# Third weight chunk split by halves, and the second batch's first exponentials ahead of a worker's step, in a kernel of attention and two layers of matmuls

## The chip, the cores and the metric

The kernel runs on one core of a Trainium2 chip. The metric is the time of one execution on the device, in microseconds (us), taken as the median of several runs. The engines are named as the profile names them: PE is TensorE (matmuls; PEld its weight loads), DVE is VectorE, ACT is ScalarE, POOL is GpSimd, SP is SyncE, which here only issues loads and stores. PSUM is the memory that PE writes its accumulators to, in banks.

## What is computed

Sparse attention (the first half of the heads local, the other half strided), then a bilinear layer, then four experts weighted by given probabilities:

```python
def _attn_ref(q, k, v):                      # (2, 8, 576, 64) each
    scores = scale * np.matmul(q, k.transpose(0, 1, 3, 2))
    mask_local = (rel >= 0) & (rel < stride)
    mask_strided = (rel >= 0) & (pos[None, :] % stride == pos[:, None] % stride)
    ...
    scores = np.where(masks[None, :, :, :], scores, -1000000000.0)
    scores = scores - np.max(scores, axis=-1, keepdims=True)
    attn = np.exp(scores)
    attn = attn / (np.sum(attn, axis=-1, keepdims=True) + 1e-09)
    return np.matmul(attn, v).astype(np.float32)

def _moe_ref(x, w1, w2, w3, w_out):          # x (1152, 512), w1, w2 (512, 1024)
    return ((x @ w1) * (x @ w2) @ w3 @ w_out).astype(np.float32)

def _moe2_ref(x, domain_probs, w1, w2):
    p = domain_probs / (domain_probs.sum(-1, keepdims=True) + 1e-09)
    for e in range(E):
        out += p[:, e:e + 1] * (np.maximum(x @ w1[e], 0.0) @ w2[e])
    return out.astype(np.float32)
```

## The kernel before

The order of the instructions on every engine is the order in which the program is written. Each engine works through its own list in that order; semaphores make an instruction wait for what it reads.

**Matmuls in pairs.** Most operands are held as a rounded high part and the rest, `w_hi` and `w_lo`, `x_hi` and `x_lo`. One product step is three matmuls (`mm3`, lines 303 to 307): high by high, high weight by low x, low weight by high x.

**Weight chunks and the worker.** The weights of the bilinear layer come in chunks of 128 x 1024 (`Chunk`; eight of w1 and w2 in `c_w12`, then w_out and w3). Each is loaded as raw 64-bit words and made into numbers in steps: `magnitude` (line 149, ACT), `clamp`, `shift`, `sign`, `add` (lines 185 to 195, DVE) with `round_up` (line 144, ACT), then `split_hi` (line 203, a cast on ACT that writes `w_hi`) and `split_lo` (line 232, a subtraction on DVE that writes `w_lo`). The add ends with the load of a later chunk into the raw buffer that it has read. A generator `work` holds these steps from the third chunk on, each chunk's split mixed with the next one's steps; `advance(1)` issues what stands up to the next `yield`. The second chunk, made outside of it, already has its add and its split by halves (`add_halves`, `low_halves`, lines 207 to 220).

**Units.** The layer's first products are made in 32 units (batch, chunk, half of the batch's 576 tokens). A unit (`ab_block`, line 586) fills two PSUM accumulators of 128 x 288, w = 0 and w = 1, of twelve matmuls each. ACT copies the first to the tile `ab` (line 609), and DVE multiplies the second by it (line 611). The accumulator w = 0 reads columns 0 to 511 of the chunk, w = 1 the others. `run_unit` (line 889) issues a unit in two blocks, one for each accumulator, and after each block one step of the worker. Units 0 and 1 are made otherwise; units 2 and 3 read the second chunk, units 4 and 5 the third, units 6 and 7 the fourth.

**The second batch's attention** runs between the units, chunk by chunk (`Chunk4`, six of them), by `attend` (line 908). For chunk s a call makes: the scores of chunk s + 1 on PE (from the fourth on; the first three were made before), the maxima of chunk s (line 409 on DVE, scaled on GpSimd, line 411), the reciprocal and multiplication of chunk s - 1 (lines 453 and 457, DVE), values and output of chunk s - 3, and the transposes of chunk s - 2 (line 462, PE, tile `tp`). The exponentials of chunk s (line 433, six or eight on ACT) are put into the list `waiting` and issued in the next unit, after its first block and the worker's step. The scores lie in three PSUM banks, so the fourth chunk's scores take over the first one's bank. Before the change, the first call comes after unit 3, the second after unit 4, the third, which has the fourth chunk's scores and the first one's transposes, after unit 5.

**The rest** of the kernel, from 62 us on, is the other units, the product of w3 and w_out, and the experts.

Of the kernel before, what the change touches and what calls it, by code (L numbers as in the profile page):

```python
# [8 lines left out]
F32 = mybir.dt.float32  # L9
# [5 lines left out]
ALU = mybir.AluOpType  # L15
# [3 lines left out]
P = 128  # L19
# [25 lines left out]
def kernel(  # L45
# [13 lines left out]
    nc = tc.nc  # L59
    mm = nc.tensor.matmul  # L60
# [13 lines left out]
    def bank(name):  # L74
        return ps.tile([P, 512], F32, tag="ps", name=name)
# [54 lines left out]
    class Chunk:  # L130
# [68 lines left out]
        def split_hi(self):  # L199
            nonlocal live  # L200
            live += 2
            self.hi, self.lo = unit("w_hi"), unit("w_lo")
            nc.scalar.copy(self.hi, self.f32)
# [5 lines left out]
        def add_halves(self):  # L209
# [3 lines left out]
            for i in range(2):  # L213
                c = slice(512 * i, 512 * i + 512)
                self.add_half(i)
                nc.scalar.copy(self.hi[:, c], self.f32[:, c])

        def low_halves(self):
            for c in (slice(0, 512), slice(512, 1024)):
                nc.vector.tensor_tensor(out=self.lo[:, c], in0=self.f32[:, c], in1=self.hi[:, c].bitcast(F32),  # L220
                                        op=ALU.subtract)
            self.done = True

        def split_half(self, i, src):
            if i == 0:
# [5 lines left out]
        def split_lo(self):  # L231
            nc.vector.tensor_tensor(out=self.lo, in0=self.f32, in1=self.hi.bitcast(F32), op=ALU.subtract)
            self.done = True
# [8 lines left out]
    c_w12 = [Chunk(w12[c]) for c in range(8)]  # L242
    c_wout = [Chunk(w_out[c]) for c in range(4)]
    c_w3 = [Chunk(w3T[c]) for c in range(8)]
    live = 6
# [6 lines left out]
    def load_next(held=False):  # L252
        nonlocal loaded
        if loaded < len(stream):
            stream[loaded].raw_load(held)
            loaded += 1
            for load in rest_loads.pop(loaded, ()):
                load()

    def work():  # L260


        wide = stream[2:20]
        before = None
        for c, after in zip(wide, wide[1:] + [None]):
            if before:
                while live > 14:
                    yield False
                before.split_hi()
            c.clamp()  # L270
            yield True
            if before:
                before.split_lo()
            c.shift()
            yield True
            c.round_up()
            c.sign()
            yield True
            if after:
                after.magnitude()  # L280
            c.add()
            yield True
            before = c
        while live > 14:
            yield False
        before.split_hi()
        yield True
        before.split_lo()
        yield True
        for w in c_e:  # L290
            yield from w.work()

    worker = work()

    def advance(n=1):

        return all([next(worker, False) for _ in range(n)])

    def need(c, part=0):
        while not (c.done if part == 0 else c.done1 if part == 1 else c.done2):  # L300
            assert advance()

    def mm3(acc, lhs, rhs, first, last):
        (lh, ll), (rh, rl) = lhs, rhs
        mm(acc, lh, rh, start=first, stop=False)  # L305
        mm(acc, lh, rl, start=False, stop=False)  # L306
        mm(acc, ll, rh, start=False, stop=last)  # L307


    x_hi = xp.tile([P, 4, NT], F32R, tag="x_hi", name="x_hi")  # L310
    x_lo = xp.tile([P, 4, NT], F32R, tag="x_lo", name="x_lo")
# [218 lines left out]
    def ab_place(b, pair):  # L530
        both = big[b].tile([P, 4 * S], F32R, tag="big", name="ab_parts")
        parts_of[b, pair] = both[:, :4 * MAIN].rearrange("p (x k n) -> p x k n", x=2, k=2)
        rest = both[:, 4 * MAIN:].rearrange("p (x n) -> p x n", x=2)
        if pair == 3 and b == 0:
            middle[pair, 0] = rest[:, :, MID // 2:]
        elif pair == 3:
            nc.scalar.copy(rest[:, :, :MID // 2], middle[pair, 0].bitcast(F32))
        middle[pair, 1 - b] = rest

    def ab_pieces(b, ft, t0, n):  # L540
        pair, k = ft // 2, ft % 2
        pieces = []
        cut = MAIN if b == 0 else MID // 2
        for a, z in ((t0, min(cut, t0 + n)), (max(cut, t0), t0 + n)):
            if a < z:
                at = slice(a - t0, z - t0)
                if (a < cut) == (b == 0):
                    off = 0 if b == 0 else cut
                    pieces.append((at, parts_of[b, pair][:, :, k, a - off:z - off]))
                else:  # L550
                    off = b * S - MAIN
                    pieces.append((at, middle[pair, k][:, :, a + off:z + off]))
        return pieces
# [32 lines left out]
    def ab_block(b, ft, n):  # L586
        t = slice(b * S + n * HB, b * S + n * HB + HB)
        pair, late = ft // 2, b == 0 and ft < 6
        ab = tmp.tile([P, HB], F32, tag="pT", name="ab")
        if n == 0 and ft % 2 == 0:  # L590
            if late:
                if pair < 2:
                    parts = big[pair].tile([P, 2, 2, S], F32, tag="big", name="ab_f32")
                    whole[pair] = parts[:, 0]
                    if pair:
                        whole[2] = parts[:, 1]
            elif (b, pair) not in parts_of:
                ab_place(b, pair)
        if late:
            full = whole[pair][:, ft % 2, n * HB:n * HB + HB]  # L600
        else:
            full = ab
            pieces = ab_pieces(b, ft, n * HB, HB)
        for w in range(2):
            acc = bank("ab_acc")[:, :HB]
            for k in range(4):
                mm3(acc, c_w12[ft].parts((w * 4 + k) * P, P), (x_hi[:, k, t], x_lo[:, k, t]), k == 0, k == 3)
            if w == 0:
                nc.scalar.copy(ab, acc)
            else:  # L610
                nc.vector.tensor_tensor(out=full, in0=acc, in1=ab, op=ALU.mult)
            yield
        if late:
            return
        split_hi(pieces, ab)
        yield
        split_lo(pieces, ab)
        yield
# [132 lines left out]
    class Step:  # L751
# [22 lines left out]
        def add(self, out, acc, b):  # L774
            nc.vector.tensor_tensor(out=out, in0=acc, in1=b, op=ALU.add)  # L775

        def first(self, work):

            n = self.half.n
# [80 lines left out]
    with tc.manual_schedule():  # L860
# [22 lines left out]
        done = 0  # L883
# [2 lines left out]

        waiting = []

        def run_unit():

            nonlocal done, rest
            b, ft, i = units[done]
            if done >= 2:
                need(c_w12[ft])
            block = ab_block(b, ft, i)
            for _ in range(2):
                next(rest, None)
                next(block)
                if done >= 2:
                    advance(1)  # L900
                if waiting:
                    waiting.pop().slots_exps()
            rest = block
            done += 1
            if b == i == 1:
                c_w12[ft].free()

        def attend(b, s):

            nonlocal live  # L910
            chunk = chunks[b]
            n = len(chunk)
            if 3 <= s + 1 < n:
                chunk[s + 1].scores()
            if s < n:
                chunk[s].maxima()
            if 1 <= s <= n:
                chunk[s - 1].recip()
                chunk[s - 1].normalise()
            if 3 <= s:  # L920
                c = chunk[s - 3]
                c.pv()
                c.put()
                c.put_lo()
                if c.g == 0:
                    live -= 1
            if 2 <= s < n + 2:
                chunk[s - 2].transposes()
                chunk[s - 2].evac(nc.scalar.copy)
            if s < n:  # L930
                waiting.append(chunk[s])
# [97 lines left out]
        for n in range(2):  # L1029
            acc = bank("ab_acc")[:, :HB]  # L1030
# [10 lines left out]
        done = 2  # L1041
        advance(4)
        steps = iter(range(9))
        while done < 16:
            if done == 3:
                need(c_w12[2])
            run_unit()
            if done in (4, 5, 6, 7, 8, 10, 11, 13, 14):
                attend(1, next(steps))
            if done == 6:  # L1050
                zero.whole_split()
# [15 lines left out]
        for it in range(8):  # L1067
# [8 lines left out]
            i = {1: 0, 3: 1, 6: 2}.get(it)  # L1076
            if i is not None:
                c = wc[i]
# [4 lines left out]
        c = None  # L1083
# [23 lines left out]
        for c in wc[:3]:  # L1107
# [6 lines left out]
        steps = [Step(half, e, c, c_e[16 * i + 4 * e + c])  # L1114
                 for i, half in enumerate(halves) for e in range(E) for c in range(4)]
# [10 lines left out]
        for s, step in enumerate(steps):  # L1126
            need(step.w, 1)
            before = steps[s - 1] if s else None
# [87 lines left out]
```

## Time and profile before

| | |
|---|---|
| median of 3 runs | 616.2 us (616.09 to 616.81) |
| the profiled execution | 618.54 us, of it 616.8 us span |
| PE, DVE, ACT busy in the span | 610.5, 442.1, 279.9 us |

The span is the time from the first to the last instruction of the profiled execution. PE's busy time is modelled from its matmuls, which overlap; a matmul of 288 columns begins about 0.13 us after the one before it and is shown with a length of 0.29. So a PE without a gap is seen from the starts, and a wait from the row of waits.

### The profile page before, as it was taken

What the parts mean: (1) busy time and instruction counts of PE and PEld (TensorE: products, weight loads), DVE (VectorE), ACT (ScalarE), POOL (GpSimd) and SP (SyncE); (2) the same over time, 40 slices, a digit from 0 to 9 for tenths busy, and PEclk for the clock granted to TensorE, in tenths of its full rate; (3) what the DMA queues carried; (4) which work ended last, traced back from release to release, by engine and by line L of the source; (5) the groups of instructions that cost most, each with busy time, mean ns of one, the idle gap of its engine ahead of it and who ended that gap; (6) DMA issues with size and microseconds to landing.
All of it is one profiled execution on the core that took longest, in us unless ns stands there. A gap on an engine that the chain in (4) does not pass through costs nothing.

```text
span 616.8 us, 11164 instructions
## 1 busy us (share of the span) xinstructions
PE 610.5 (99%) x4488; PEld 557.0 (90%) x4488; DVE 442.1 (72%) x805; ACT 279.9 (45%) x562; POOL 16.2 (3%) x45
## 2 busy tenths in 40 slices
PE   8999999999999999999999999999999999999997
PEld 5789999998889999999899998999889898989996
DVE  4799977999753227777877987887766665755843
ACT  4769966776743134333343433434343333333320
POOL 4102200000000000000000000000000000000000
PEclk9899999999999999999999999999999999999999
DMA  8987340245412201333445344435585557464411
GB/s 264 319 299 210 135 143 2 82 157 201 176 68 94 85 28 69 137 138 136 192 158 193 121 158 168 167 144 205 184 324 196 214 193 249 162 234 175 153 53 69
DMA packets 28314, 99.48 MB, mean 161 GB/s; under 512 B 2630, under 2 KB 6158, under 8 KB 25830
## 3 DMA queue, kind: packets, MB, share of 16 engines
q1 hardware_dynamic: 27718, 98.17, 44.6%
q8 instruction: 35, 0.57, 0.4%
q10 hardware_dynamic: 544, 0.59, 0.3%
q14 instruction: 17, 0.14, 0.1%
HBM read 79.62 MB, written 19.14 MB: 160 GB/s over the span
## 4 chain that ended last, share of the span: by engine, by line
PE 98%; DMA 1%; issue 0%; ACT 0%; DVE 0%; ACTq 0%
PE g_acc L305 11%; PE g_acc L306 11%; PE g_acc L307 11%; PE ab_acc L305 5%; PE ab_acc L307 5%; PE ab_acc L306 5%; PE m_a L307 4%; PE m_a L306 4%; PE m_a L305 4%; PE m_b L306 3%; PE m_c L305 3%; PE m_b L305 3%; PE m_c L306 3%; PE x_acc L305 3%; PE m_c L307 3%; PE m_b L307 3%
## 5 line engine op out<-in xcount | busy, mean ns | idle before, releaser
L769 ACT ACTIVATE h_hi<-u 128x320 fp32r<-128x320 f32 (+1 forms) x128 | 56.9, 445 | 189.2 <-DVE u L775 189.2
L305 PE MATMUL g_acc<-w_hi,h_hi 128*128 128x512 f32 (+1 forms) x296 | 114.3, 386 | 0.0
L306 PE MATMUL g_acc<-w_lo,h_hi 128*128 128x512 f32 (+1 forms) x296 | 114.2, 386 | 0.0
L307 PE MATMUL g_acc<-w_hi,h_lo 128*128 128x512 f32 (+1 forms) x296 | 113.7, 384 | 0.0
L708 DVE TENSOR_TENSOR w_lo<-raw,w_hi 128x768 fp32r<-128x768 f32 x64 | 69.5, 1086 | 12.4 <-ACT w_hi L706 12.3
L775 DVE TENSOR_TENSOR u<-m_b,u 128x320 f32<-128x320 f32 (+1 forms) x96 | 40.8, 453 | 50.1 <-PE m_b L307 50.1
L305 PE MATMUL ab_acc<-x_hi,w_hi 128*128 128x288 f32 x240 | 71.4, 297 | 0.0
L307 PE MATMUL ab_acc<-x_hi,w_lo 128*128 128x288 f32 x240 | 70.7, 295 | 0.0
L306 PE MATMUL ab_acc<-x_lo,w_hi 128*128 128x288 f32 x240 | 70.7, 294 | 0.0
L307 PEld LDWEIGHTS g_acc<-w_hi,h_lo 128*128 128x128 f32 x296 | 55.6, 188 | 11.6
L305 PEld LDWEIGHTS g_acc<-w_hi,h_hi 128*128 128x128 f32 x296 | 55.8, 188 | 8.0
L306 PEld LDWEIGHTS g_acc<-w_lo,h_hi 128*128 128x128 f32 x296 | 55.8, 188 | 7.6
L771 DVE SCALAR_TENSOR_TENSOR h_lo<-u,h_hi 128x320 fp32r<-128x320 f32 (+1 forms) x128 | 57.9, 452 | 3.6 <-ACT h_hi L769 1.4
L706 ACT CAST w_hi<-raw 128x768 fp32r<-128x768 f32 x64 | 59.9, 936 | 0.0
L305 PEld LDWEIGHTS ab_acc<-x_hi,w_hi 128*128 128x128 f32 x240 | 45.0, 188 | 0.1
L306 PEld LDWEIGHTS ab_acc<-x_lo,w_hi 128*128 128x128 f32 x240 | 45.0, 188 | 0.0
L307 PEld LDWEIGHTS ab_acc<-x_hi,w_lo 128*128 128x128 f32 x240 | 45.0, 188 | 0.0
L306 PE MATMUL m_b<-b_t,s_hi 128*128 128x320 f32 (+1 forms) x128 | 37.9, 296 | 0.0
L775 DVE TENSOR_TENSOR u<-m_a,u 128x320 f32<-128x320 f32 (+1 forms) x64 | 28.9, 452 | 11.6 <-PE m_a L307 11.6
L708 DVE TENSOR_TENSOR s_lo<-raw,s_hi 128x1024 fp32r<-128x1024 f32 x16 | 19.6, 1226 | 24.3 <-ACT s_hi L706 24.3
L775 DVE TENSOR_TENSOR u<-m_c,u 128x320 f32<-128x320 f32 (+1 forms) x64 | 29.1, 454 | 4.5 <-PE m_c L307 3.9
L785 ACT COPY u<-m_a 128x320 f32<-128x320 f32 (+1 forms) x32 | 12.8, 399 | 42.1 <-PE m_a L307 42.1
(182 smaller groups left out, 1396.4 us busy)
## 6 DMA issues: line engine op xcount, KB each, us to landing
raw<-in_e_dram SPq DMA_DIRECT2D x32, 1024.0 KB, 4.9
raw<-in_w3T_dram SPq DMA_DIRECT2D x8, 1024.0 KB, 4.9
stored<-s_hi SPq DMA_DIRECT2D x16, 512.0 KB, 2.6
stored<-s_lo SPq DMA_DIRECT2D x16, 512.0 KB, 2.7
s_hi<-stored SPq DMA_DIRECT2D x16, 512.0 KB, 3.7
s_lo<-stored SPq DMA_DIRECT2D x16, 512.0 KB, 5.4
raw<-in_w_dram SPq DMA_DIRECT2D x7, 1024.0 KB, 7.8
raw<-in_w_out_dram SPq DMA_DIRECT2D x4, 1024.0 KB, 5.0
```

Source lines behind the costliest of these rows:

```text
L305: mm(acc, lh, rh, start=first, stop=False)
L306: mm(acc, lh, rl, start=False, stop=False)
L307: mm(acc, ll, rh, start=False, stop=last)
L706: nc.scalar.copy(dst[0], src)
L708: nc.vector.tensor_tensor(out=dst[1], in0=src, in1=dst[0].bitcast(F32), op=ALU.subtract)
L769: nc.scalar.activation(hi, src, AF.Relu)
L771: nc.vector.scalar_tensor_tensor(out=lo, in0=src, scalar=0.0, in1=hi.bitcast(F32), op0=ALU.max, op1=ALU.subtract)
L775: nc.vector.tensor_tensor(out=out, in0=acc, in1=b, op=ALU.add)
L785: nc.scalar.copy(u1, a)
```

## The change

Three things change. The third chunk, `wide[0]` in the worker, gets its add, its cast and its subtraction by halves, like the second one; the casts are issued with the add, and no longer one step later; the subtraction's first half comes ahead of the fourth chunk's clamp, its second half where the whole one was. The first accumulator of unit 4, the first to read the third chunk, makes its eight matmuls with `w_hi` first and its four with `w_lo` last. And the first call of `attend` for the second batch moves from the end of unit 3 into its second block, ahead of the worker's step; its exponentials are issued right after that step, in the same block.

```diff
+        def low_half(self, i):
+            c = slice(512 * i, 512 * i + 512)
+            nc.vector.tensor_tensor(out=self.lo[:, c], in0=self.f32[:, c], in1=self.hi[:, c].bitcast(F32),
+                                    op=ALU.subtract)
+            self.done = i == 1
...
+            first_wide = before is wide[0]
+            if before and not first_wide:
                 while live > 14:
                     yield False
                 before.split_hi()
+            if first_wide:
+                before.low_half(0)
             c.clamp()
             yield True
-            if before:
+            if first_wide:
+                before.low_half(1)
+            elif before:
                 before.split_lo()
...
-            c.add()
+            if c is wide[0]:
+                while live > 14:
+                    yield False
+                c.add_halves()
+                load_next()
+            else:
+                c.add()
...
+    def high_first(acc, pairs):
+        for i, ((lh, _), (rh, rl)) in enumerate(pairs):
+            mm(acc, lh, rh, start=i == 0, stop=False)
+            mm(acc, lh, rl, start=False, stop=False)
+        for i, ((_, ll), (rh, _)) in enumerate(pairs):
+            mm(acc, ll, rh, start=False, stop=i == len(pairs) - 1)
...
+            if (b, ft, n, w) == (0, 2, 0, 0):
+                high_first(acc, [(c_w12[ft].parts((w * 4 + k) * P, P), (x_hi[:, k, t], x_lo[:, k, t]))
+                                 for k in range(4)])
...
-        def run_unit():
+        def run_unit(between=None):
...
-            for _ in range(2):
+            for i_half in range(2):
                 next(rest, None)
                 next(block)
+                if between and i_half:
+                    between()
                 if done >= 2:
                     advance(1)
...
+        def begin():
+            attend(1, next(steps))
+
         while done < 16:
             if done == 3:
                 need(c_w12[2])
-            run_unit()
-            if done in (4, 5, 6, 7, 8, 10, 11, 13, 14):
+            run_unit(begin if done == 3 else None)
+            if done in (5, 6, 7, 8, 10, 11, 13, 14):
                 attend(1, next(steps))
```

ACT's list, from the fourth chunk's magnitude (`t_741` is that chunk, `t_734` the third; `w_hi_771` the third's cast and `w_hi_846` the fourth's, `ab_756`, `ab_791`, `ab_830` the copies of units 2, 3 and 4; `p_ring_158,rec_850<-sc_649` the six exponentials), before:

```order
L149 ACTIVATE t_741<-raw64_611 128x1024
L609 COPY ab_756<-ab_acc_757 128x288
L203 CAST w_hi_771<-t_734 128x1024
L609 COPY ab_791<-ab_acc_792 128x288
L144 ACTIVATE raw64_611<-raw64_611 128x1024
L149 ACTIVATE t_822<-raw64_729 128x1024
L609 COPY ab_830<-ab_acc_832 128x288
L203 CAST w_hi_846<-t_741 128x1024
L433 ACTIVATE p_ring_158,rec_850<-sc_649,mx_827 128x64 x6
L609 COPY ab_879<-ab_acc_880 128x288
```

The same stretch of ACT's list after the change:

```order
L149 ACTIVATE t_741<-raw64_611 128x1024
L216 CAST w_hi_743<-t_734 128x512 x2
L635 COPY ab_761<-ab_acc_762 128x288
L635 COPY ab_794<-ab_acc_795 128x288
L144 ACTIVATE raw64_611<-raw64_611 128x1024
L149 ACTIVATE t_828<-raw64_729 128x1024
L455 ACTIVATE p_ring_158,rec_833<-sc_649,mx_825 128x64 x6
L635 COPY ab_841<-ab_acc_843 128x288
L203 CAST w_hi_857<-t_741 128x1024
L635 COPY ab_882<-ab_acc_883 128x288
```

The third chunk's casts moved ahead of unit 2's copy, and the six exponentials ahead of unit 4's copy and of the fourth chunk's cast.

DVE's list from the product of unit 3 to the first chunk's multiplication by its reciprocals (`ab_f32` are the products, `w_lo_847` the fourth chunk's subtraction, `mx` the maxima of the attention's chunks), before:

```order
L611 TENSOR_TENSOR ab_f32_623<-ab_acc_808,ab_791 128x288
L195 ISA t_741<-raw64_611,t_741 128x2048
L409 TENSOR_REDUCE mx_827<-sc_649 128x6
L185 TENSOR_SCALAR t_822<-t_822 128x1024
L611 TENSOR_TENSOR ab_f32_831<-ab_acc_858,ab_830 128x288
L232 TENSOR_TENSOR w_lo_847<-t_741,w_hi_846 128x1024
L188 TENSOR_SCALAR t_822<-t_822 128x1024
L409 TENSOR_REDUCE mx_874<-sc_675 128x6
L453 RECIPROCAL rec_850<-rec_850 128x6
L457 TENSOR_TENSOR p_ring_158<-p_ring_158,rec_850 128x384
```

And after the change:

```order
L637 TENSOR_TENSOR ab_f32_623<-ab_acc_811,ab_794 128x288
L431 TENSOR_REDUCE mx_825<-sc_649 128x6
L195 ISA t_741<-raw64_611,t_741 128x2048
L185 TENSOR_SCALAR t_828<-t_828 128x1024
L637 TENSOR_TENSOR ab_f32_842<-ab_acc_861,ab_841 128x288
L236 TENSOR_TENSOR w_lo_858<-t_741,w_hi_857 128x1024
L188 TENSOR_SCALAR t_828<-t_828 128x1024
L431 TENSOR_REDUCE mx_877<-sc_675 128x6
L475 RECIPROCAL rec_833<-rec_833 128x6
L479 TENSOR_TENSOR p_ring_158<-p_ring_158,rec_833 128x384
```

Only the first maxima moved, by one place, ahead of the fourth chunk's add.

DVE's list a little earlier, from the third chunk's sign step to the fourth chunk's, after the change (`t_734` is the third chunk, `t_741` the fourth):

```order
L191 SCALAR_TENSOR_TENSOR t_734<-raw64_527,t_734 128x1024
L207 ISA t_734<-raw64_527,t_734 128x1024 x2
L220 TENSOR_TENSOR w_lo_744<-t_734,w_hi_743 128x512
L185 TENSOR_SCALAR t_741<-t_741 128x1024
L637 TENSOR_TENSOR ab_f32_623<-ab_acc_778,ab_761 128x288
L220 TENSOR_TENSOR w_lo_744<-t_734,w_hi_743 128x512
L188 TENSOR_SCALAR t_741<-t_741 128x1024
L191 SCALAR_TENSOR_TENSOR t_741<-raw64_611,t_741 128x1024
```

Before, one whole add and one whole subtraction stood there, the subtraction where its second half stands now.

## Rows read from the trace of the kernel before

**Rows 1.** The page's busy line: us, share of the span, instructions.

```profile
PE 610.5 (99%) x4488; PEld 557.0 (90%) x4488; DVE 442.1 (72%) x805; ACT 279.9 (45%) x562; POOL 16.2 (3%) x45
```

**Rows 2.** PE's longest wait (total, times, longest) and its timeline (start, length).

```profile
PE o L483 <- issue: 1.4, 1, 1.4
...
18.67 0.42 PE L483 MATMUL o<-pT,tv_loc 64*64 64x32 f32 x11 [1.39 <-issue]
```

**Rows 3.** Busy time by stretch: length, engines, granted clock, DMA share, GB/s.

```profile
50.74:613.55 562.81, 562.81 (x3665) 519.00 (x3663) 403.61 (x738) 247.84 (x487) 5.35 (x9) 1.00 0.41 150
```

**Rows 4.** PE's timeline: start, length, line, output<-inputs, shape, count.

```profile
43.12 0.29 PE L305 MATMUL ab_acc<-x_hi,w_hi 128*128 128x288 f32 x1
...
43.37 0.30 PE L307 MATMUL ab_acc<-x_hi,w_lo 128*128 128x288 f32 x1
...
49.51 0.34 PE L396 MATMUL sc<-m_str,i_str 128*128 128x432 bf16 x1
...
50.74 0.55 PE L462 MATMUL tp<-ident,p_ring 128*128 128x128 f32 x3
```

**Rows 5.** DVE's timeline, in the same columns.

```profile
32.57 1.29 DVE L207 CUSTOM_DVE_ANT_0 t<-raw,t 128x1024 uint16<-128x1024 uint16 x2
...
39.42 1.23 DVE L195 CUSTOM_DVE_ANT_0 t<-raw,t 128x2048 uint16<-128x2048 uint16 x1
...
41.77 1.23 DVE L232 TENSOR_TENSOR w_lo<-t,w_hi 128x1024 fp32r<-128x1024 f32 x1
...
44.77 0.45 DVE L611 TENSOR_TENSOR ab_f<-ab_acc,ab 128x288 f32<-128x288 f32 x1
45.14 1.22 DVE L195 CUSTOM_DVE_ANT_0 t<-raw,t 128x2048 uint16<-128x2048 uint16 x1
46.27 0.55 DVE L409 TENSOR_REDUCE mx<-sc 128x6 f32<-128x384 f32 x1
46.74 0.68 DVE L185 TENSOR_SCALAR t<-t 128x1024 f32<-128x1024 f32 x1
47.34 0.45 DVE L611 TENSOR_TENSOR ab_f<-ab_acc,ab 128x288 f32<-128x288 f32 x1
47.71 1.22 DVE L232 TENSOR_TENSOR w_lo<-t,w_hi 128x1024 fp32r<-128x1024 f32 x1
48.84 0.69 DVE L188 TENSOR_SCALAR t<-t 128x1024 int32<-128x1024 int32 x1
49.44 0.55 DVE L409 TENSOR_REDUCE mx<-sc 128x6 f32<-128x384 f32 x1
49.91 0.18 DVE L453 RECIPROCAL rec<-rec 128x6 f32<-128x6 f32 x1
50.12 0.56 DVE L457 TENSOR_TENSOR p_ring<-p_ring,rec 128x384 f32<-128x384 f32 x1
```

**Rows 6.** ACT's timeline; a bracket gives the idle time before and its releaser.

```profile
33.29 1.22 ACT L216 CAST w_hi<-t 128x512 fp32r<-128x512 f32 x2 [1.03 <-DVE t L207]
...
44.89 0.40 ACT L609 COPY ab<-ab_acc 128x288 f32<-128x288 f32 x1 [0.68 <-PE ab_acc L307]
...
46.39 1.05 ACT L203 CAST w_hi<-t 128x1024 fp32r<-128x1024 f32 x1 [1.10 <-DVE t L195]
47.57 0.32 ACT L433 ACTIVATE p_ring<-sc,mx 128x64 f32<-128x64 f32 x1
...
49.33 0.42 ACT L609 COPY ab<-ab_acc 128x288 f32<-128x288 f32 x1
49.61 1.20 ACT L144 ACTIVATE raw<-raw 128x1024 int32<-128x1024 uint32 x1
```

**Rows 7.** GpSimd's timeline.

```profile
46.91 0.62 POOL L411 TENSOR_SCALAR mx<-mx 128x6 f32<-128x6 f32 x1 [27.01 <-DVE mx L409]
```

**Rows 8.** Busy time by stretch, as in rows 3, of two early stretches.

```profile
16.88:20.29 3.41, 2.02 (x89) 1.70 (x81) 2.63 (x7) 1.90 (x5) 2.11 (x6) 1.00 0.92 273
20.29:23.71 3.42, 3.42 (x56) 3.03 (x49) 1.47 (x3) 1.56 (x5) 0.00 (x0) 0.50 0.84 335
```

More of the change, by code (lines that the diff above doesn't have):

```diff
@@ L216, in add_halves @@
                 nc.scalar.copy(self.hi[:, c], self.f32[:, c])
+        def low_half(self, i):
[3 more added lines that the diff above has]
+            self.done = i == 1
         def low_halves(self):
[L219 to L222, printed above, removed]
+            for i in range(2):
+                self.low_half(i)
         def split_half(self, i, src):
@@ L269, in work @@
                 before.split_hi()
+            if first_wide:
+                before.low_half(0)
             c.clamp()
             yield True
-            if before:
+            if first_wide:
+                before.low_half(1)
+            elif before:
                 before.split_lo()
@@ L605, in ab_block @@
             acc = bank("ab_acc")[:, :HB]
-            for k in range(4):
-                mm3(acc, c_w12[ft].parts((w * 4 + k) * P, P), (x_hi[:, k, t], x_lo[:, k, t]), k == 0, k == 3)
+            if (b, ft, n, w) == (0, 2, 0, 0):
+                high_first(acc, [(c_w12[ft].parts((w * 4 + k) * P, P), (x_hi[:, k, t], x_lo[:, k, t]))
+                                 for k in range(4)])
+            else:
+                for k in range(4):
+                    mm3(acc, c_w12[ft].parts((w * 4 + k) * P, P), (x_hi[:, k, t], x_lo[:, k, t]), k == 0, k == 3)
             if w == 0:
```

## Prediction

> **What bounds the kernel now.** I read the page's busy line first, then the waits of the tensor engine (PE), then its busy time over the long stretch, and last, engine by engine, the 20 us that the diff touches. The busy line has PE at 610.5 of 616.8 us [rows 1]; its longest wait of the whole run is 1.4 us, and that one ends at 18.67, in the first batch's attention [rows 2]. From 50.74 us to its last matmul PE is busy for 562.81 of 562.81 us [rows 3]. So a microsecond that PE loses near 50 us is not given back later, and nothing can be won there by making another engine earlier, unless PE waits for it.
>
> In the stretch of the change PE does not wait either, but it is closely followed by the vector engine (DVE). The reader should see three near misses in the rows. The third weight chunk's low half (w_lo) is written from 41.77 for 1.23, so until 43.00, and the first matmul that reads it starts at 43.37 [rows 4, 5]. The six exponentials of the second batch's first attention chunk are over when the scalar engine (ACT) begins its next copy at 49.33; the scores that take over their bank begin at 49.51 [rows 4, 6]. And the normalised probabilities are written until 50.12 + 0.56 = 50.68, and PE begins to transpose them at 50.74 [rows 4, 5]. The third one decides here: nothing lies between them, so every delay of DVE up to that multiplication is a delay of PE.
>
> **The halves of the third chunk.** The add in two pieces takes 1.29 us against 1.23 for the whole one, both shapes standing in the trace (32.57, of the chunk before, and 39.42) [rows 5]; the cast of such a pair starts 0.72 after its add starts and takes 1.22 [rows 5, 6]. With the add at 39.42 as before, the casts run from 40.14 to 41.36. DVE waits for the first (until about 40.8), writes half a w_lo (about 0.60) to 41.44, clamps (0.60) to 42.04, multiplies the a and b blocks (0.37) to 42.41 and writes the other half to 43.01. That is where the whole w_lo ended before; from the w_lo's start the next product came 3.00 later (41.77 to 44.77), of which 1.14 was the w_lo [rows 5], so the next product comes at 42.41 + 0.60 + 1.86 = 44.87, 0.10 later than before. What PE gets: the first w_hi half at 40.8 and the first w_lo half at 41.5 for a block that starts at 43.12 [rows 4]; its first accumulation reads only these halves. The 0.37 us of margin become more than 1.5, but a margin is all that it was: gain 0. The reordered matmuls are the same twelve, same shape: 0. Nor does it matter whether a wait is for a half or for the whole tile: the whole w_hi is there at 41.4, and the last of w_lo at 43.1, ahead of the second accumulation, which starts at 43.12 plus twelve matmuls at 0.125 (43.12 to 43.37 is two), 44.6. One ACT copy, of an accumulator of the unit before, is now queued behind the two casts and starts at about 41.3; it takes 0.4, and its reader on DVE, the product, comes at 42.04, so that costs nothing.
>
> **The maxima and exponentials ahead of the worker's step.** On DVE the maxima swap places with the whole add of chunk four. On ACT the six exponentials now stand ahead of a copy of the product accumulator (before at 44.89) and of chunk four's cast (before at 46.39) [rows 6]. That is the step that costs. I follow the chain row by row:
>
> - product at 44.87; 0.37 on [rows 5], maxima from 45.24 to 45.79 (0.55). Before, GpSimd took the maxima 0.09 after their end, needed 0.62, and ACT began 0.04 later [rows 5 to 7]; so the first exponential is at 46.54, where it was at 47.57.
> - The six took from 47.57 to 49.33, 1.76 us [rows 6]. They end at 48.30. So far a gain of 1.0 us, and the scores' bank at 49.51 has over 1 us of margin.
> - Only now comes the copy: 48.30, 0.42 long, done at 48.72, where before it was done at 45.3. DVE has meanwhile done the add (1.13) and the clamp (0.60) and is ready for the product at 45.71 + 1.13 + 0.60 = 47.44, nearly when it was before (47.34); but the product reads the copy, so it waits until 48.76: 1.3 us of idle DVE where there was none.
> - The cast of chunk four follows the copy (0.28 from start to start) [rows 6]: 48.58 to 49.63. DVE is free at 49.13 and waits for it, another 0.54, until 49.67.
> - From here DVE's order is the old one, at the old pitches: w_lo 1.13, shift 0.60, second maxima 0.47, reciprocal 0.21, multiplication 0.56 long [rows 5]. That gives 50.80, 51.40, 51.87, 52.08 and an end at 52.64. The transposes on PE follow 0.06 later, at **52.70 instead of 50.74**.
>
> PE's order around it is unchanged: scores of the fourth chunk, then these transposes, then the next block. It stands still for 1.96 us, and nothing after it has slack to take that back [rows 3]. Chunk four's w_lo, now done at 50.9, is needed only after the transposes, so it is covered by the same hole; had the transposes not been late, it would have been a near miss of its own (its block stands right behind these transposes). The loads: chunk four's add releases a raw buffer 0.6 later than before, and the load that takes it has PE's two microseconds as cover. No queue gets an instruction more, apart from three half-size ones on DVE and ACT in place of whole ones. GpSimd does the same list in the same order.
>
> Bounds of this term: if the first GpSimd instruction took half of its 0.62, the chain ends 0.3 earlier, 1.6 us; if the six exponentials or the cast run longer as neighbours change, some 0.4 more, 2.4 us. Below zero it can't go in this profile, since PE waits for nothing there; the value that I take is the chain's, 2.0.
>
> **The sum.** Halves 0, matmul order 0, exponentials +2.0: the span goes from 616.8 to 618.8, and the profiled execution, 618.54, to 620.5. The three runs have their median at 616.2, 2.3 us below the profiled one; I add the same term to it: 618.2, or 0.33% more.
>
> **Rivals.** *The clock falls in the hole* (619.9). In this trace PE was busy for 2.02 of 3.41 us in a stretch of small matmuls with a hole of 1.4 us in it [rows 2, 8], and for the 3.42 us behind it the granted clock was 0.50, the 1.2 GHz level [rows 8]. The new hole is longer, with scores in small matmuls ahead of it; a fall of that length in dense matmuls costs half of it, 1.7 us, so 618.2 + 1.7. Against it speaks that dense 288-column matmuls stand on both sides, which the early stretch had not. The Trainium skill (TensorE: Matmul & The Clock Gate, the part on the HAM clock gate) says that the low clock is TensorE's resting state and that activity releases it, so that a hole can cost more than its own length; the trace agrees in the stretch just named.
>
> *The hole is there before, too, or is covered* (616.2, no change). Without the profiler the run is 2.3 us shorter, and where it loses them I can't see. If PE comes to the transposes 2 us later against DVE than the profile shows, DVE's delay is hidden. For it: only one execution is profiled. Against it: the products at 44.77 and 47.34 [rows 5] read PE's accumulators, so a PE that came 2 us later would hold DVE up too; and if PE came earlier instead, the chain on DVE would set the time of the transposes in both kernels, with the same difference.
>
> *Faster* (615.2). The mechanism is the exponentials' earlier end. The transposes hang on them too: they are over about 49.4, GpSimd scales their sums, and the reciprocal follows on DVE at 49.91 [rows 5, 6]. If in undisturbed runs it is ACT that is late there, PE waits for it now, for the scores' bank and again for the transposes, and the change gives it the 1.0 us worked out above. It decides only from the point where ACT's chain is later than DVE's by more than DVE's new delay, 2.0; in the profile the two meet within 0.1 and PE shows no wait for either.
>
> *The change doesn't do what it says*: if the half dependencies fell together to whole tiles, nothing is lost, as worked out above; it gives the main case's time.
>
> **How the numbers follow.** Main case, 618.2 (from 617.8 to 618.8 with the bounds and the spread of the three runs): 0.62. Clock falls, 619 to 620: 0.15. Partly or wholly covered, 616 to 617.2: 0.17. Faster: 0.06. The range leaves out the faster case and most of the covered one: 616.9 to 619.9. A measurement of this kernel tells about 0.2%, 1.2 us, from no change. Slower by more than that takes the main case and the clock, less a little for a term at its lower bound: 0.75; within it 0.20; faster by more 0.05.
>
> **What would show it.** In the profile after: a wait of PE at the transposes of about 2 us, ended by DVE's multiplication, near 50.7; on DVE an idle of 1.3 us ahead of a product ended by an ACT copy, and one of 0.5 ahead of a w_lo ended by the cast; on ACT an idle of about 2 us ahead of the first exponential while a finished accumulator lies uncopied. The scores of the fourth chunk begin without a wait, and the matmuls of chunk three too. I am wrong if PE goes from the scores to the transposes without a hole, or if PE shows waits around 43 or 49.5 that the profile before did not show.

## The result, and the profile after

The change makes the kernel slower: 622.55 us (median of 5 runs, 621.36 to 622.86) against 616.81 for the kernel before in the same comparison (5 runs), a ratio of 1.0088 with a 95% interval of 1.0074 to 1.0101. That is 5.7 us where the prediction had 2.0, and 622.55 lies outside its range of 616.9 to 619.9. The direction was right and the size was not.

The busy line of the page after; the span of this execution is 620.9 us, where it was 616.8:

```profile
PE 610.5 (98%) x4488; PEld 557.2 (90%) x4488; DVE 442.9 (71%) x807; ACT 280.1 (45%) x563; POOL 17.2 (3%) x45
```

PE does the same 4488 matmuls in the same 610.5 us as in [rows 1]. What grew is its idle time. Its waits after (releaser: total, times, longest):

```profile
PE tp L484 <- DVE p_ring L479: 3.0, 1, 3.0
PE sc L418 <- ACT p_ring L455: 1.3, 1, 1.3
```

The kernel before waits at neither place (its longest wait is the one in [rows 2]); the first is the predicted hole, half as long again. PE's timeline there (start, length, line, output<-inputs, and in brackets the idle time before and its releaser):

```profile
47.53 0.29 PE L322 MATMUL ab_acc<-x_hi,w_lo 128*128 128x288 f32 x1
49.11 0.34 PE L418 MATMUL sc<-m_str,i_str 128*128 128x432 bf16 x1 [1.29 <-ACT p_ring L455]
49.38 1.01 PE L425 MATMUL sc<-tqk 64*54 64x54 f32 x32
53.37 0.81 PE L484 MATMUL tp<-ident,p_ring 128*128 128x128 f32 x3 [2.98 <-DVE p_ring L479]
53.83 0.59 PE L320 MATMUL ab_acc<-x_hi,w_hi 128*128 128x288 f32 x1
54.22 0.44 PE L321 MATMUL ab_acc<-x_lo,w_hi 128*128 128x288 f32 x1
54.46 0.44 PE L322 MATMUL ab_acc<-x_hi,w_lo 128*128 128x288 f32 x1
```

The last three rows show a third thing: behind the hole the matmuls start 0.39 and 0.24 apart, where 0.13 is usual. The stretches after the hole (length, busy time of PE, PEld, DVE, ACT and POOL, granted clock, DMA share, GB/s):

```profile
53.51:56.92 3.41, 3.41 (x16) 3.41 (x16) 3.38 (x6) 3.41 (x13) 1.26 (x2) 0.50 0.03 5
56.92:60.00 3.08, 3.08 (x76) 2.81 (x79) 2.91 (x5) 3.08 (x14) 0.00 (x0) 1.00 0.98 324
```

For 3.41 us the granted clock was 0.50, the 1.2 GHz level. The other engines explain the hole. DVE after, in the stretch of [rows 5]:

```profile
44.45 0.45 DVE L637 TENSOR_TENSOR ab_f<-ab_acc,ab 128x288 f32<-128x288 f32 x1
44.82 0.55 DVE L431 TENSOR_REDUCE mx<-sc 128x6 f32<-128x384 f32 x1
45.28 1.22 DVE L195 CUSTOM_DVE_ANT_0 t<-raw,t 128x2048 uint16<-128x2048 uint16 x1
46.42 0.68 DVE L185 TENSOR_SCALAR t<-t 128x1024 f32<-128x1024 f32 x1
49.38 0.46 DVE L637 TENSOR_TENSOR ab_f<-ab_acc,ab 128x288 f32<-128x288 f32 x1 [2.28 <-ACT ab L635]
50.33 1.23 DVE L236 TENSOR_TENSOR w_lo<-t,w_hi 128x1024 fp32r<-128x1024 f32 x1 [0.49 <-ACT w_hi L203]
...
52.75 0.56 DVE L479 TENSOR_TENSOR p_ring<-p_ring,rec 128x384 f32<-128x384 f32 x1
```

GpSimd, which scales the maxima between DVE and the exponentials, and ACT:

```profile
45.46 1.68 POOL L433 TENSOR_SCALAR mx<-mx 128x6 f32<-128x6 f32 x1 [24.81 <-DVE mx L431]
49.22 0.25 POOL L458 TENSOR_SCALAR rec<-rec 128x6 f32<-128x6 f32 x1 [2.07 <-ACT p_ring L455]
```

```profile
47.18 0.32 ACT L455 ACTIVATE p_ring<-sc,mx 128x64 f32<-128x64 f32 x1 [3.23 <-POOL mx L433]
...
48.93 0.42 ACT L635 COPY ab<-ab_acc 128x288 f32<-128x288 f32 x1
49.21 1.09 ACT L203 CAST w_hi<-t 128x1024 fp32r<-128x1024 f32 x1
```

The reader is to see one row above all. The scaling of 6 numbers per partition, 0.62 in [rows 7], took 1.68, from 45.46 to 47.14. In that time DVE ran the fourth chunk's add and its clamp, and the clamp ended at 46.42 + 0.68 = 47.10. A sister instruction at 49.22, while DVE was idle or read PSUM, took 0.25.

### The profile page after: what moved, and what is told of

The parts are those of the page before. It is cut to its first block, busy times and chain, and to the rows that moved or that the text cites. A ratio compares the mean times of both kernels' runs of the same rounds, so it can differ in the third digit from the quotient of the medians.

```text
span 620.9 us, 11168 instructions
## 1 busy us (share of the span) xinstructions
PE 610.5 (98%) x4488; PEld 557.2 (90%) x4488; DVE 442.9 (71%) x807; ACT 280.1 (45%) x563; POOL 17.2 (3%) x45
## 4 chain that ended last, share of the span: by engine, by line
PE 92%; DVE 3%; DMA 2%; ACT 1%; issue 1%; POOL 0%; DVEq 0%; POOLq 0%
PE g_acc L320 11%; PE g_acc L321 11%; PE g_acc L322 11%; PE ab_acc L320 5%; PE ab_acc L321 5%; PE ab_acc L322 5%; PE m_a L322 4%; PE m_a L321 4%; PE m_a L320 4%; PE m_b L321 3%; PE m_c L320 3%; PE m_c L321 3%; PE m_b L320 3%; PE x_acc L320 3%; PE m_c L322 3%; PE m_b L322 3%
```

## The experiments

All ratios are against the kernel before, run on the same chip.

**Is the early clock fall of [rows 8] part of the kernel, or of that one execution?** The kernel before once more, unchanged.

> The kernel before, unchanged, for a second profile of it. In its first profile the granted clock was 0.50 from 20.3 to 23.7 us, and PE began unit 2 at 36.6; in the profile after the change there was no such fall early and PE began unit 2 at 34.8. Theory A (the early fall was particular to that one execution): without it PE begins unit 2 near 34.8 to 35, and since DVE is no earlier, PE now waits, up to 1.8 us in all, at the third chunk's w_lo, at the scores or at the transposes; the time stays at 616.1 to 617.2. Theory B (the kernel before always has the early fall): unit 2 begins at 36.6 again and PE shows no wait over 0.1 us after 25 us.

Measured: 617.23 us (10 runs), ratio 0.9999 (0.9985 to 1.0013), span 615.2. The clock did not fall early, and PE came to the transposes at 49.19 instead of 50.74:

```profile
47.97 0.34 PE L396 MATMUL sc<-m_str,i_str 128*128 128x432 bf16 x1
49.19 0.55 PE L462 MATMUL tp<-ident,p_ring 128*128 128x128 f32 x3
```

DVE came as much earlier, against what I had expected; the multiplication, which ended at 50.68 in [rows 5], now ended at 49.14:

```profile
48.58 0.56 DVE L457 TENSOR_TENSOR p_ring<-p_ring,rec 128x384 f32<-128x384 f32 x1
```

The profile that the prediction used had a fall of its own in it. From the transposes to the end both take the same: 616.8 - 50.74 = 566.06 and 615.2 - 49.19 = 566.01. This makes a yardstick for every kernel below: its span is the start of these transposes plus 566.0, and what is above that was lost behind them.

**Do the halves cost anything?** Only they remain; the first call of `attend` goes back behind unit 3.

```diff
-            run_unit(begin if done == 3 else None)
-            if done in (5, 6, 7, 8, 10, 11, 13, 14):
+            run_unit()
+            if done in (4, 5, 6, 7, 8, 10, 11, 13, 14):
```

> The change without its second part: third chunk by halves and high matmuls first, but the first maxima and exponentials where they were. Theory A (the loss comes from the exponentials ahead of the copy on ACT): as before within 0.2%, 615.6 to 617.6, perhaps up to 1 us faster if PE waits for w_lo in the kernel before; no wait of PE at the transposes over 1 us. Rival B (the halves, which queue unit 2's copy behind the casts, cost too): slower than 618.

Measured: 616.93 us (10 runs), ratio 0.9997 (0.9984 to 1.0010), span 615.1, transposes at 49.12. The halves cost and gain nothing, alone.

**Does the earlier begin carry all of it?** Only it remains: the third chunk's steps whole, unit 4's matmuls in the old order.

```diff
-            first_wide = before is wide[0]
+            first_wide = False
...
-            if c is wide[0]:
+            if False:
...
-            if (b, ft, n, w) == (0, 2, 0, 0):
+            if False:
```

> The change without its first part: third chunk as before, the first maxima and exponentials ahead of the worker's step. Theory A: the whole loss, 621.5 to 623; first GpSimd scaling about 1.7 long, under the fourth chunk's add and clamp on DVE; PE waits near 3 us at the transposes, ended by DVE's multiplication, and 1 us or more at the scores. Rival B: less than half of the loss, under 619.5, with the rest in the halves.

Measured: 621.43 us (8 runs), ratio 1.0066 (1.0044 to 1.0088), span 618.1, transposes at 52.08 behind a wait of 2.94. The hole belongs to the earlier begin. The wait of 1 us at the scores that I had expected did not come.

**What is the part of GpSimd in the hole?** The first chunk's maxima are scaled on ACT, right ahead of the exponentials, all else as in the changed kernel.

```diff
-            if self.b:
+            if self.b and self.index:
                 nc.gpsimd.tensor_scalar_mul(mx[:, :s], mx[:, :s], -SCALE)
...
-            if not self.b:
+            if not self.b or not self.index:
                 nc.scalar.activation(self.mx[:, :self.slots], self.mx[:, :self.slots], AF.Copy, scale=-SCALE)
```

> The whole change, but the first chunk's maxima are scaled on ACT, which is idle there, in place of GpSimd. Theory A (GpSimd's 1.68 us is time in which it is held up by DVE's add and clamp; the queue order on ACT is the rest): the first exponential begins 0.3 to 0.4 after the maxima end in place of 1.8, PE's wait at the scores is gone, its wait at the transposes is about 1.5 us in place of 3.0, and the time 619.0 to 620.5, some 0.8 less if no fall of the clock follows the shorter hole. Rival B (GpSimd's length is no part of the chain, the copy behind the exponentials is all): both waits as after, 621.5 to 623.

Measured: 618.78 us (8 runs), ratio 1.0026 (1.0007 to 1.0045), span 616.6. ACT's new instruction, DVE's two waits and PE's:

```profile
44.16 0.21 ACT L452 ACTIVATE mx<-mx 128x6 f32<-128x6 f32 x1 [1.48 <-DVE mx L431]
```

```profile
46.61 0.46 DVE L637 TENSOR_TENSOR ab_f<-ab_acc,ab 128x288 f32<-128x288 f32 x1 [0.74 <-ACT ab L635]
47.56 1.23 DVE L236 TENSOR_TENSOR w_lo<-t,w_hi 128x1024 fp32r<-128x1024 f32 x1 [0.49 <-ACT w_hi L203]
```

```profile
50.60 0.55 PE L484 MATMUL tp<-ident,p_ring 128*128 128x128 f32 x3 [1.44 <-DVE p_ring L479]
```

The hole went from 2.98 to 1.44, and DVE's wait for the copy from 2.28 to 0.74: both lost 1.54, which is GpSimd's 1.69 and its handover less ACT's 0.24. So about half of the hole passes through GpSimd, and the other half is the order on ACT.

**Which of the two waits of PE is the change's?** The changed kernel again, unedited.

> The changed kernel, unchanged, for a second profile of it. In its first profile the second chunk came late (DVE began its clamp at 28.07, against 26.8 to 26.9 in the four runs since), PE waited 1.29 us at the scores and 2.98 at the transposes, and the granted clock fell behind the second hole. Theory A (the hole is the 2.9 us of the run with the second part alone; the wait at the scores belongs to the late chunk): with the clamp near 26.8, PE's wait at the scores is under 0.2, at the transposes 2.9 to 3.0, and the span 618.0 without a fall of the clock, 619.4 to 619.8 with one. Rival B (the two parts together cost more than the second alone): waits over 1 us at the scores and 3 at the transposes again with the clamp at 26.8.

Measured: 622.69 us (5 runs, 619.76 to 623.74), ratio 1.0102 (1.0085 to 1.0119). Its profile is of the 619.76 run, span 618.0, with neither a wait at the scores nor a fall of the clock:

```profile
47.71 0.34 PE L418 MATMUL sc<-m_str,i_str 128*128 128x432 bf16 x1
47.98 1.01 PE L425 MATMUL sc<-tqk 64*54 64x54 f32 x32
51.97 0.55 PE L484 MATMUL tp<-ident,p_ring 128*128 128x128 f32 x3 [2.98 <-DVE p_ring L479]
```

The 2.98 is the same, and so is GpSimd's 1.69. The 1.29 at the scores, one of the "waits around 43 or 49.5" by which the prediction was to be known as wrong, comes from elsewhere: in the profile after, a load of the second chunk landed late. Here are ACT's and DVE's rows of it, then the same rows of the run now:

```profile
26.90 1.14 ACT L149 ACTIVATE t<-raw 128x1024 f32<-128x1024 f32 x1 [1.32 <-DMA raw<-in_w_dram]
28.07 0.69 DVE L185 TENSOR_SCALAR t<-t 128x1024 f32<-128x1024 f32 x1 [1.77 <-ACT t L149]
```

```profile
25.46 1.17 ACT L149 ACTIVATE t<-raw 128x1024 f32<-128x1024 f32 x1
26.66 0.69 DVE L185 TENSOR_SCALAR t<-t 128x1024 f32<-128x1024 f32 x1 [0.37 <-ACT t L149]
```

28.07 - 26.66 is 1.41, and everything on DVE up to the transposes is that much later (53.37 against 51.97).

**Is it the order on ACT?** Maxima early as in the change, exponentials where they were, behind unit 4's copy and the cast.

```diff
-                if waiting:
+                if waiting and not between:
                     waiting.pop().slots_exps()
```

> The whole change, but the first exponentials stay where they were on ACT, behind unit 4's copy and the fourth chunk's cast; only the maxima are early. Theory A (the loss is ACT's order): GpSimd's first scaling is again about 1.7 us long, but what follows it on ACT no longer delays the cast, and PE's waits at the scores and at the transposes are under 0.3 us; time 616.2 to 617.3. Rival B (the hold of GpSimd or the maxima's place costs by itself): a wait of 1 us or more, over 618.

Measured: 617.86 us (10 runs), ratio 1.0020 (1.0002 to 1.0038), but the profiled execution had the late load of the second chunk (1.87 on ACT), and so a wait of 1.90 at the scores and a fall of the clock. It answers the question only in part: the transposes had no wait. So the same kernel was run a second time.

> The change with the first exponentials left behind copy and cast, a second look. In its first profile the second chunk was late (DVE's clamp at 28.12) and PE waited 1.9 us at the scores. Theory A (that wait was the late chunk's): with the clamp near 26.8 the waits of PE at the scores and transposes are under 0.3 us each and the run lies at 616.3 to 617.4. Rival B (the held GpSimd delays the exponentials in this order too): a wait of 1 us or more at the scores with the clamp at 26.8.

Measured: 617.51 us (10 runs), ratio 1.0006 (0.9996 to 1.0015), span 615.2, clock 0.999 to 1.0 in all ten. GpSimd, and PE:

```profile
43.94 1.69 POOL L433 TENSOR_SCALAR mx<-mx 128x6 f32<-128x6 f32 x1 [23.11 <-DVE mx L431]
```

```profile
47.89 0.34 PE L418 MATMUL sc<-m_str,i_str 128*128 128x432 bf16 x1 [0.17 <-ACT p_ring L455]
49.15 0.55 PE L484 MATMUL tp<-ident,p_ring 128*128 128x128 f32 x3
```

GpSimd is held for the same 1.69, until 45.63, and it costs nothing measurable. The copy and the cast that DVE waits for stand ahead of the exponentials in this order, and the cast ends later than GpSimd, at 46.07:

```profile
45.01 1.06 ACT L203 CAST w_hi<-t 128x1024 fp32r<-128x1024 f32 x1 [1.64 <-DVE t L195]
```

**The copy or the cast?** The exponentials stand between them: behind unit 4's copy, ahead of the cast.

```diff
                 if between and i_half:
                     between()
+                if waiting and done == 4:
+                    waiting.pop().slots_exps()
...
-                if waiting:
+                if waiting and not between:
```

> The whole change, but the exponentials come behind unit 4's copy and still ahead of the fourth chunk's cast. My prediction put most of DVE's delay (1.3 of 1.9 us) on the copy. Theory A (it is the cast that counts: copy and cast both wait for the exponentials, and DVE's subtraction waits for the cast whether or not the product before it is early): PE's wait at the transposes is 2.6 to 2.8 us in place of 2.9. Rival B (the copy counts): under 1.5 us.

Measured: 620.97 us (4 runs), ratio 1.0065 (1.0050 to 1.0081), span 618.2. The product came on time, at 44.69, and DVE's next wait was all the longer:

```profile
47.70 1.23 DVE L236 TENSOR_TENSOR w_lo<-t,w_hi 128x1024 fp32r<-128x1024 f32 x1 [2.56 <-ACT w_hi L203]
```

```profile
50.74 0.90 PE L484 MATMUL tp<-ident,p_ring 128*128 128x128 f32 x3 [2.68 <-DVE p_ring L479]
```

Taking the copy out of the queue gives back 0.3 of 2.98. It is the cast behind the exponentials that makes the hole; the copy only stood in front of it.

**What holds GpSimd?** The maxima one step earlier, ahead of the fourth chunk's sign step instead of its add, so that a single DVE instruction with two operands in SBUF follows, and then the product, which reads PSUM.

```diff
-                if between and i_half:
+                if between and not i_half:
```

> The whole change, but the first maxima come one worker step earlier, ahead of the fourth chunk's sign step on DVE (two operands in memory, 1.22 us) in place of its add and clamp; the exponentials then stand ahead of the fifth chunk's magnitude on ACT too. What holds GpSimd up? Theory A1 (any DVE instruction that reads two operands from SBUF, or runs in a faster mode): GpSimd's first scaling ends with the sign step, 1.0 to 1.2 us long. Theory A2 (only the faster modes, as tensor_scalar and the add; the sign step, which needs 1.2 ns an element, does not): 0.25 us. Chain in both: exponentials ahead of magnitude, copy and cast; wait of PE at the transposes 1.8 us by A1 and 1.0 by A2; time 618.3 to 620 or 617.5 to 619. Rival B (GpSimd is just slow to start after an idle time of over 20 us, whatever DVE does): 1.7 us long again, and the wait at the transposes 2.3 or more.

Measured: 620.15 us (4 runs), ratio 1.0055 (1.0036 to 1.0074). GpSimd and DVE:

```profile
42.66 1.16 POOL L433 TENSOR_SCALAR mx<-mx 128x6 f32<-128x6 f32 x1 [21.76 <-DVE mx L431]
```

```profile
42.02 0.55 DVE L431 TENSOR_REDUCE mx<-sc 128x6 f32<-128x384 f32 x1
42.48 1.22 DVE L191 SCALAR_TENSOR_TENSOR t<-raw,t 128x1024 int32<-128x1024 int32 x1
43.62 0.45 DVE L637 TENSOR_TENSOR ab_f<-ab_acc,ab 128x288 f32<-128x288 f32 x1
```

GpSimd ended at 43.82, 0.12 after the sign step (43.70), and no longer waited for a second instruction. Its time follows the DVE instruction beside it; a slow start after long idle, the rival, would have given 1.7 again.

**Does the fall of the clock come from the hole?** Twenty matmuls of 288 columns into the still unused tile `tp`, ahead of the transposes, fill it; nothing reads them.

```diff
+            if self.b and not self.index:
+                for _ in range(20):
+                    mm(self.tp[:, :HB], x_hi[:, 0, :P], x_hi[:, 0, :HB], start=True, stop=True)
```

> The whole change, with twenty matmuls of 288 columns added on PE between the fourth chunk's scores and the first chunk's transposes, about 2.7 us that nobody reads, in the hole of 2.98 us; the transposes write over them. Nine of ten runs of the changed kernel lie at 621.4 to 623.7 with a mean granted clock of 0.994 to 0.997, one at 619.76 with 0.999. Theory A (the hole costs its own length and then a fall of the granted clock behind it, of which the matmuls in the hole rid us): PE's wait at the transposes falls to about 0.3 us, they start when they did, and most runs lie at 619.3 to 620.3 with a clock of 0.999 or 1.0; median about 2.5 below the changed kernel. Rival B (the falls have nothing to do with the hole): the hole is filled all the same, the median stays at 622 to 623 and the clock at 0.994 to 0.997.

Measured: 621.07 us (6 runs, 618.92 to 621.92), ratio 1.0056 (1.0040 to 1.0073), span 618.0, clock 0.999 to 1.0 in all six:

```profile
48.94 2.90 PE L485 MATMUL tp<-x_hi 128*128 128x288 f32 x20
51.99 0.55 PE L487 MATMUL tp<-ident,p_ring 128*128 128x128 f32 x3
```

No run shows a fall, and the lateness is still there: the transposes start at 51.99, as without the filling (51.97). The median is 3.9 us over the kernel before on the same chip, where the changed kernel was 5.7 over it both times; but it is above the 619.3 to 620.3 that was expected of it, since four of the six runs lie at 620.95 to 621.92 with a full clock. Why those are later is open.

One rival stays. The changed kernel itself was not run on the chip of this experiment, and on that chip none of 33 runs of any kernel shows a clock under 0.999. The kernel with the exponentials in place had 4 of 10 low runs on another chip and 0 of 10 on this one. So the filling and the chip are not told apart.

Start of the transposes, what PE waited ahead of them, and the span less that start, by profiled execution (us):

| kernel | transposes | wait | rest | runs at a clock of 0.997 or less |
|---|---|---|---|---|
| before, rerun | 49.19 | none | 566.0 | 0 of 10 |
| halves only | 49.12 | none | 566.0 | 2 of 10 |
| exponentials in place, rerun | 49.15 | none | 566.1 | 0 of 10 |
| exponentials in place, first | 51.52 | 1.90 at the scores | 566.7 | 4 of 10 |
| maxima scaled on ACT | 50.60 | 1.44 | 566.0 | 3 of 8 |
| maxima ahead of the sign | 51.04 | 1.84 | 567.6 | 3 of 4 |
| exponentials behind the copy | 50.74 | 2.68 | 567.5 | 4 of 4 |
| begin only | 52.08 | 2.94 | 566.0 | 6 of 8 |
| changed, rerun | 51.97 | 2.98 | 566.0 | 4 of 5 |
| changed, first profile | 53.37 | 2.98 | 567.5 | 5 of 5 |
| hole filled | 51.99 | none | 566.0 | 0 of 6 |

A rest of 567.5 is one fall of the clock at the hole: 1.5 us (in the first run with the exponentials in place it began ahead of the transposes, so part of it lies there). Besides the profile after, three profiles of the table show one, and each begins in its hole or less than 0.4 us behind it. These are the stretches of two of them, of the exponentials behind the copy and of the maxima ahead of the sign, with the columns of the stretches shown for the profile after:

```profile
50.46:53.88 3.42, 3.14 (x14) 3.14 (x15) 3.42 (x6) 3.42 (x15) 1.03 (x2) 0.50 0.02 5
```

```profile
51.39:54.80 3.41, 3.41 (x16) 3.41 (x15) 3.35 (x6) 3.41 (x12) 1.27 (x2) 0.50 0.11 22
```

Of the runs without a profile only the mean clock is known, and not where it fell. Without a hole a low clock is rarer: of 57 runs of the kernel before beside these experiments 3 were at 0.997, and 2 of 10 with the halves only. By the mean clock of a run, 3.41 us at 0.50 are worth 1.7 of 618, so 0.997; the runs at 0.994 and 0.995 lost about twice that.

## Why the prediction went wrong, point by point

**Right: what bounds the kernel.** The transposes behind DVE's normalisation were the place, and what PE lost there nothing gave back: the rest is 566.0 with a hole ahead of it as without one.

**Right: the halves.** Predicted 0; alone they measure 0.9997 (0.9984 to 1.0010). The product behind them was to come 5.45 after the third chunk's add begins (39.42 to 44.87); in the profile after it came at 44.45, with the add at 39.03: 5.42.

**Wrong, the failed step: "GpSimd took the maxima 0.09 after their end, needed 0.62".** It needed 1.68, so the term that I put at 2.0 for the exponentials' move is 1.0 larger. I took the duration from [rows 7], as if it belonged to the instruction, and bounded it only downwards, by "if the first GpSimd instruction took half of its 0.62". But the 0.62 was itself a wait: in [rows 5] DVE's clamp runs from 46.74 to 47.42, and GpSimd, 46.91 to 47.53, ends 0.11 after it. The change puts the scaling beside the add and the clamp, and it waited for both, 0.04 past the clamp's end. The expensive neighbour was in the order of instructions from the start: maxima, add, clamp. The Trainium skill (SBUF — State Buffer, the section on SBUF's two separate sides) states the rule that I missed: VectorE and GpSimd take turns at a shared pair of ports, held for a whole instruction, when VectorE's instruction runs in a two-port mode or reads two operands from SBUF while GpSimd reads SBUF. The trace agrees: 1.69 beside the add and the clamp, 1.16 beside the sign step, 0.25 where DVE ran nothing of the kind. Add and sign step read two operands from SBUF; that the clamp, which reads one, runs in a two-port mode stands in no row. That GpSimd was not let in between the add and the clamp is what the runs show here.

From this one term the rest follows at the predicted pitches. In times from the third chunk's add:

| step | predicted | after |
|---|---|---|
| GpSimd begins | 6.46 | 6.43 |
| first exponential | 7.12 | 8.15 |
| unit 4's copy | 8.88 | 9.90 |
| transposes | 13.28 | 14.34 |

All after the first row are late by 1.02 to 1.06. The hole, 1.96 predicted, is 2.98.

**Right in the sum, wrong in the reason: "the product reads the copy, so it waits until 48.76: 1.3 us", and "another 0.54" for the cast.** Both waits are there (2.28 and 0.49, the first with GpSimd's microsecond in it). But with the copy out of the way the hole shrinks by only 0.3: the cast, 0.28 behind it, holds DVE just as long.

**Wrong in its chance, the second step that failed: "The clock falls in the hole" (0.15).** It was the likeliest case. Of 10 runs of the changed kernel 9 have a mean clock of 0.997 or less, and in the profile after the fall cost 1.5, near the 1.7 worked out. What I held against it, dense matmuls on both sides, does not protect: they stood on both sides, with only the scores' small matmuls in between, at the holes of 1.84, 2.68 and 2.98 us where the profiles show a fall. The two errors add up. With a hole of 2.98 the main case comes to 619.2, still inside the range; with the fall of 1.5 it is 620.7, outside of it. The Trainium skill's rule that the prediction named (TensorE: Matmul & The Clock Gate, the part on the HAM clock gate), that the low clock is the resting state, agrees with these rows as far as they go: low at the holes, full in the runs with the hole filled.

**The base.** The profile of before held an early fall that its rerun does not, and PE's margin at the third chunk's `w_lo` looked wider than it is. In the rerun, unit 4's wait for the third chunk's `w_lo` and the scores' wait together are some 0.4 us, too small for rows of their own and seen only from the matmuls' starts. The changed kernel begins the scores 0.26 earlier than the rerun (47.71 against 47.97), and so a hole of 2.98 makes 2.8 in the span (615.2 to 618.0). Alone such a gain wins nothing, since the transposes wait for DVE's normalisation: its multiplication ends 0.05 ahead of them in the rerun (49.14, 49.19).

**The sum as it was.** In the profile after, against the rerun of the kernel before, 2.8 for the hole, 1.4 for the late load and 1.5 for the fall make the whole difference of the spans, 615.2 to 620.9. The median's 5.7 is not taken apart in this way: the hole and one fall make 4.3 of it, and for the other 1.4 two things in the records have the size, a late load and a second fall in the runs at 0.994 and 0.995 (2 of the first 5, 2 more in the rerun). Why the second chunk's load is late in some executions stays open, and no run here tells whether the change makes it more frequent; the runs of the kernel before at a full clock spread by as much, from 614.3 to 616.7 in span.

No version beat the kernel before. The two that come level, the halves alone and the exponentials in place in their second run (1.0020 in the first), show that there was next to nothing to win here.

## What to carry to other kernels

Before an instruction is moved, look at which instruction of the other engine it will run beside: here a tiny GpSimd operation took as long as the DVE instructions on SBUF that it met, so its duration in the trace was its neighbour's and not its own. When a chain is moved forward on an engine that works in order, price it by what it pushes back, and test each of the pushed ones by itself (here the cast counted, and not the copy that the waits named). And a hole on a dense TensorE is to be priced with a fall of the clock: in this kernel most runs with holes of 1.8 to 3 us show a low mean clock, and one fall cost 1.5 us more.

## What the runs showed of the hardware that I had not expected

GpSimd is held through two DVE instructions in a row: 1.69 for add and clamp, 1.16 for the sign step, 0.25 alone. TensorE's granted clock fell to 0.50 for 3.4 us at holes of 1.84 to 2.98 us in otherwise dense matmuls, in four profiles; 22 of 26 runs of the kernels with a hole of this size at the transposes have a mean clock of 0.997 or less, and none of 6 with the hole filled by unread matmuls, on a chip without any low run. And one load landed late in one execution, so that all of DVE's work behind it came 1.4 us later than in another and PE waited some 20 us after it.
